# Four more chunks whose activations are turned by DMA: attention with pooled keys, then a mixture of adapters, on one core

## The chip, the cores and the metric

The kernel runs on 1 core of one Trainium2 chip. The metric is device microseconds (us) of that core, from one launch. The kernel before took 378.78 us, the median of 3 runs (378.42 to 379.87 us).

## The reference

Two stages follow each other. `q` has the shape (4, 12288, 128), `kv` (4, 384, 32, 128); the output has 49152 rows of 128.

```python
kv_pool = kv.reshape(B, H//4, 4, W//4, 4, C).mean(axis=(2, 4))   # 768 pooled rows per batch
k = v = kv_pool.reshape(B, -1, C) @ w_sr
a = softmax((q @ k.T) / sqrt(C))
x = (a @ v).reshape(B * S, D)                                    # stage 1
logits = x @ w_gate                                              # 8 experts, the top 2 of them
w = softmax over the two chosen logits
out = x + sum over the two chosen e of  w_e * (x @ A[e]) @ B[e]  # A: 128 x 16, B: 16 x 128
```

## The kernel before, in words

**Chunks and slots.** The 49152 queries are cut into 96 chunks of 512 (24 per batch). The main loop (lines 588 to 699) makes one pass per chunk; such a pass is called a slot here, and slot k is the pass with that value of `k`. The program keeps the order in which the code issues instructions on each engine, so the order in the code is the order in every queue. Several chunks are under way in a slot:

- three calls of `unit()`, the scores of chunk k (line 288): two matmuls of 512 columns each into PSUM, then one exponential on ScalarE (ACT);
- `attend` for chunk k-1 (line 306): 24 matmuls of 136 columns;
- `normalize` for chunk k-2 (line 323): a reciprocal and one multiplication on VectorE (DVE) give the rows `xn`; `top` and `route` start the choice of experts on DVE and GpSimd (POOL), and `gates` (line 373) ends it with a tanh on ACT and two products on POOL, `gw`;
- for an earlier chunk, found in `enter[k]`: `down` (line 427, four matmuls of 128 columns, `h_ps`, whose weights are the turned x), then `gate` (line 432, DVE, the gated activations `hg`);
- for the chunks in `ku`: `up` (line 441, four matmuls, `d_ps`, whose weights are the turned gated activations) and `finish` (line 450, an addition on DVE and the store to HBM, issued by SyncE, SP).

**Three ways to turn x and the gated activations.** Both products need their chunk with features on the partitions.

1. On TensorE (PE): `transposes` (line 381) uses four matmuls for x and four for the activations into one PSUM tile `tt_ps`, and DVE copies it to SBUF (`tts`, line 399).
2. `turn_h_dma` (line 422): the activations alone, by a DMA from `hs` to `ht`. The chunks in `by_queue` (line 542) take this way: the odd ones from 9 to 61. Their `up` comes six slots after their `gate` (line 677).
3. `turn_dma` (line 415), for the chunks in `by_dma` (line 338), 68 to 89: POOL narrows x to bf16 (`narrow`, line 412) in the slot in which the chunk is normalized, SP issues a DMA that turns it, and `down` uses it at the start of the slot two later. From the second chunk on the same DMA also turns the activations of another chunk. Slots in which the entering chunk is of this kind run through lines 604 to 636, which have no x transposes.

`by_dma` starts at `TURN` (line 336). Chunks before `TURN` are routed in pairs, those from `TURN` on one by one (`sizes`, line 337).

**The SP queue** issues, in the order of the code: the loads of `kv` (`load_kv`, line 97), the turning loads of the queries (`load_qT`, line 86: a DMA that turns 2048 rows of bf16 from HBM into SBUF, named `qT` or, for the last four groups, `qTs`), the stores of the output, and the DMAs of ways 2 and 3. SP handles them one after another. The queries in bf16 come from `cast_q` (line 79), a DMA from HBM to HBM that POOL issues. The slots of casts and query loads are written out by hand: `casts` (line 480, the groups 4 to 23 in order) and `loads` (line 481, slot to group; a group is 4 chunks, so group 17 holds the chunks 68 to 71). An odd slot with a `by_queue` chunk issues its load after that chunk's DMA (line 678), another slot just after its first `unit()` (line 601).

**PSUM.** `tt_ps`, `h_ps`, `d_ps` and the keys' tiles share two banks (`ps_m`, line 65).

**Other work in these slots.** The keys and values of the next batch are pooled by POOL (`add_patches`, line 495, at the end of the slots in `adds_at`) and made by the steps in `rest`, one per slot in which line 683 says so; for the last batch the last three are in the slots 69, 70 and 71. The kvr buffers of the pool `kvpool` also hold the last query groups and the strips of way 3 (`strip`, line 405).

Of the kernel before, what the change touches and what calls it, by code (L numbers as in the profile page):

```python
# [20 lines left out]
def kernel(  # L21
# [25 lines left out]
    NCHUNK = B * NB  # L47
# [21 lines left out]
    def mm(*a, **k):  # L69
        return keep(nc.tensor.matmul(*a, **k))  # L70
# [235 lines left out]
    def attend(k, s):  # L306
        b = k // NB
        if s == 0:
            acc[k] = ps_a.tile([P, S, 256], FP32, tag="acc", name="acc")
        o = acc[k][:, s, 0:VE]  # L310
        for j in range(J):
            mm(o, em[k][:, s, j], vx[b][:, j, 0:VE], start=(j == 0),
               stop=(j == J - 1))
# [19 lines left out]

    SOLO, TURN = NCHUNK - 6, NCHUNK - 28
    sizes = [1, 1] + [2] * (TURN // 2 - 1) + [1] * (NCHUNK - TURN)
    by_dma = range(TURN, SOLO)
    first, size = {}, {}
# [5 lines left out]
    def top(k):  # L345
        k0, m = first[k], k - first[k]
        if m == 0:
            srt[k0] = rpool.tile([P, GC, S, 8], FP32, tag="srt", name="srt")
        for s in range(S):
            keep(nc.vector.max(srt[k0][:, m, s], xn[k][:, s, C:C + E]))  # L350
# [3 lines left out]
    def route(k0):  # L354
        n = size[k0] * S
        eng = nc.gpsimd if k0 > 1 else nc.vector
        lg = xg[k0].rearrange("p m s c -> p (m s) c")[:, 0:n, C:C + E]
        so = srt[k0].rearrange("p m s e -> p (m s) e")[:, 0:n]

        def over(i):  # L360
            d = rpool.tile([P, GC * S, 8], FP32, tag=f"over{i}", name=f"over{i}")[:, 0:n]
            keep(eng.tensor_tensor(  # L362
                d, lg, so[:, :, i].unsqueeze(2).broadcast_to([P, n, 8]), op=ALU.subtract))
            return d

        arg, mask = over(0), over(1)
        keep(eng.tensor_tensor(arg, arg, mask, op=ALU.add))
        keep(eng.tensor_scalar(mask, mask, 0.0, None, op0=ALU.is_ge))  # L368


        later.append(lambda: gates(k0, n, eng, arg, mask))
# [55 lines left out]
    def down(k):  # L427
        hp[k] = mtile([P, S, P], name="h_ps")
        for s in range(S):
            mm(hp[k][:, s], xT[k][:, s], a_bf, start=(s == 0), stop=(s == S - 1))  # L430
# [44 lines left out]
    def unit(k=None, r=None):  # L475
        k, r = units.pop(0 if k is None else units.index((k, r)))
        scores(k, r)

    sums, rest = [], []
    casts = [8, 12, 15, 18, 20, 23, 26, 28, 31, 33, 36, 39, 41, 44, 46, 49, 51, 54, 57, 60]  # L480
    loads = {4 * g - 6: g for g in range(4, 18)}
    loads.update({57: 20, 59: 21, 61: 22, 64: 18, 65: 23, 66: 19})
    assert len(casts) == B * NG - 4

    rows_at, adds_at = {}, {}
    for b in range(2, B):
        for n in range(12):
            h, r, t = n // 4, n % 4, b * NB - 33 + 2 * n
# [6 lines left out]
    def add_patches(b, h, step, x):  # L495
        t = kvr[b, h]
        if step < 3:
            u, v = t[:, 0, x], t[:, step + 1, x]
        else:
            w = 2 * C if step == 3 else C  # L500
            u, v = t[:, 0, :, 0:w], t[:, 0, :, w:2 * w]
        keep(nc.gpsimd.tensor_tensor(u, u, v, op=ALU.add))  # L502

    def begin(k, queries=True):
        nonlocal sums, rest
        b, i = divmod(k, NB)
        g = k // GC
        if k in loads and queries:
            load_qT(loads[k])
        if k in casts:  # L510
            cast_q(4 + casts.index(k))
        if k in rows_at:
            load_kv(*rows_at[k], None)
        if i == 0 and 0 < b < B - 1:
            rest = prepare(b + 1, nc.gpsimd)[1]
        if k == 3:
            sums, rest = prepare(1, nc.gpsimd)
            sums = sum(sums, [])
        if 3 <= k < 15:
            load_kv(1, (k - 3) // 4, (k - 3) % 4, None)  # L520
        if k == 7:
            for _ in range(2):
                sums.pop(0)()

    def tanhs():
        while later:
            later.pop(0)()
# [7 lines left out]
    enter, t, left = {}, 1, list(range(NCHUNK - 3))  # L535
# [3 lines left out]
        left = [k for k in left if k not in enter[t]]  # L539
        t += 1  # L540

    by_queue = [k for t in range(13, TURN - 2) for k in enter[t] if k % 2]
    late_up = {}

    kh, ku, kd, kdone = [], [], [], []
# [42 lines left out]
    for k in range(k1, NCHUNK):  # L588
        b, i = divmod(k, NB)
        ka = att.get(k, [])  # L590
        kx = enter.get(k, [])
        begin(k, False)

        def after_norm(kn):
            top(kn)
            if kn == first[kn] + size[kn] - 1:
                route(first[kn])

        kn = [n for n in att.get(k - 1, []) if normed[n] == k]
        unit()  # L600
        if k in loads and not any(x_ in by_queue for x_ in kx):
            load_qT(loads[k])
        ku = ku + late_up.pop(k, [])
        if kx and not kd and all(x_ in by_dma for x_ in kx):
            down(kx[0])
            todo = []
            for n in kn:
                normalize(n)
                if n in by_dma:
                    narrow(n, k)  # L610
                    todo = [(xT, n)]
            tanhs()
            for h_ in kh:
                if h_ not in by_dma:
                    transposes(None, h_, nc.vector)
            unit()
            gate(kx[0], strip(k, 0)[:, 1])
            todo.append((hgT, kx[0]))
            if len(kx) == 1:
                turn_dma(k, *todo)  # L620
            for u_ in ku:
                up(u_)
                finish(u_)
            attend(ka[0], 0)
            attend(ka[0], 1)
            unit()
            for n in kn:
                after_norm(n)
            attend(ka[0], 2)
            for x_ in kx[1:]:  # L630
                down(x_)
                gate(x_, strip(k, 0)[:, 0])
                turn_dma(k, (hgT, x_), *todo)
            attend(ka[0], 3)
            kh, ku = kx, [c for c in kh if c not in by_queue]
            continue
        tanhs()
        for x_ in kd:
            down(x_)
        for n in kn:  # L640
            normalize(n)
            if n in by_dma:
                narrow(n, k)
                turn_dma(k, (xT, n))
        px = [c for c in kx if c not in by_dma]
        ph = [c for c in kh if c not in by_dma and c not in by_queue]
        pairs = [(px[j] if j < len(px) else None, ph[j] if j < len(ph) else None)
                 for j in range(max(len(px), len(ph)))]
        for x_, h_ in pairs[:1]:
            transposes(x_, h_, nc.vector)  # L650
        for x_ in kd:
            gate(x_)
        unit()
        for u_ in ku:
            up(u_)
            finish(u_)
        for a_ in ka[:-1]:
            for s in range(S):
                attend(a_, s)
            normalize(a_)  # L660
            after_norm(a_)
        if ka and len(ka) == 1:
            attend(ka[0], 0)
        for n in kn:
            after_norm(n)
        if k >= 13:
            unit()
            n0 = 1
        else:
            attend(ka[0], 1)  # L670
            n0 = 2
        for x_ in kx[:1]:
            down(x_)
            if x_ in by_queue:
                gate(x_, hpool.tile([P, S, P], BF16, tag="hs", name="hs"))
                turn_h_dma(x_)
                late_up[k + 6] = [x_]
                if k in loads:
                    load_qT(loads[k])
            else:  # L680
                gate(x_)
        kd = []
        if rest and i in ((14, 15, 16, 18, 19, 20, 21, 22, 23) if b == 0 else (5, 6, 7, 13, 14, 15, 21, 22, 23)):
            rest.pop(0)()
        for a_ in ka[-1:]:
            for s in range(n0 if len(ka) == 1 else 0, S):
                if s == S - 1:
                    for x_, h_ in pairs[1:]:
                        transposes(x_, h_, nc.scalar)
                        kd = [x_] if x_ is not None else []  # L690
                attend(a_, s)
        ku = [c for c in kh if c not in by_queue]
        kh = kx[:1] + kdone
        kdone = kd
        if k % 2 == 0 and 8 <= k <= 20:
            for _ in range(4 if k == 18 else 3):
                sums.pop(0)()
        for w in adds_at.get(k, []):
            add_patches(*w)
# [181 lines left out]
```

## Time and profile before

| what | before |
|---|---|
| median of 3 runs | 378.78 us |
| the profiled execution: its own time | 378.59 us |
| its span, first to last instruction | 376.8 us |
| busy share of TensorE, VectorE, ScalarE, GpSimd | 97%, 80%, 78%, 58% |
| mean granted TensorE clock | 0.993 |
| DMA moved | 85.75 MB, mean 228 GB/s |

The profile comes from one execution. Its span leaves out 1.8 us of the execution's own time, which lie before the first and after the last instruction. A page gives the busy time of each engine, the chain of work that ended last, and groups of instructions by line. The timeline lists single instructions of an engine with their start and duration in us; the windows view gives one row for a stretch. "SPq" rows are DMA issues by SyncE: the duration is that of the issue, not of the transfer. "PE" rows that overlap are pipelined, so the distance between two starts tells what a group costs.

### The profile page before, as it was taken

The page shows a single profiled execution, that of the slowest core. Times are in us where ns is not written, and L with a number is a line of the kernel's source. Part 1 is how long each engine was busy: PE and PEld are TensorE (multiplying, and loading weights), DVE is VectorE, ACT ScalarE, POOL GpSimd, SP SyncE. Part 2 cuts the span into 40 slices and gives each one's busy share as a digit, 9 for nine tenths or more (in the row PEclk, how much of TensorE's full clock was granted, in tenths as well). Part 3 has the DMA queues.
Part 4 walks back from the last instruction along what each step waited for, and adds up shares of the span by engine and source line. Part 5 has one row for each costly group of instructions (what it writes and reads, how often), then busy time and mean ns, then how long its engine had stood idle before and what let it go on. Part 6 is the DMA issues. An engine that isn't in the chain of part 4 may idle for free.

```text
span 376.8 us, 11335 instructions
## 1 busy us (share of the span) xinstructions
PE 365.9 (97%) x4340; PEld 287.5 (76%) x4340; DVE 300.5 (80%) x925; ACT 293.6 (78%) x368; POOL 218.2 (58%) x493
## 2 busy tenths in 40 slices
PE   8899999999999999999999999999999999999993
PEld 5667788877788787877877787787877777777782
DVE  1446799888888888888888888898898777777785
ACT  1548986787878788788878868877878999999873
POOL 0120368888766566557557566755645666666452
PEclk9999999999999999999999999999999999999997
DMA  8979669999999999999999999999875686777523
GB/s 255 397 261 218 231 176 271 298 268 255 240 288 265 185 288 312 182 241 294 240 259 249 287 275 203 204 257 243 211 211 156 169 170 170 169 151 186 143 88 139
DMA packets 66311, 85.75 MB, mean 228 GB/s; under 512 B 42736, under 2 KB 43504, under 8 KB 65904
## 3 DMA queue, kind: packets, MB, share of 16 engines
q1 hardware_dynamic: 62656, 73.29, 70.0%
q0 software_dynamic: 3168, 11.54, 18.2%
q8 instruction: 34, 0.56, 0.6%
q10 hardware_dynamic: 432, 0.20, 0.2%
q14 instruction: 21, 0.17, 0.2%
HBM read 50.53 MB, written 36.70 MB: 232 GB/s over the span
## 4 chain that ended last, share of the span: by engine, by line
PE 88%; DMA 6%; DVE 3%; ACT 1%; issue 1%; POOL 0%; SPq 0%; ACTq 0%; POOLq 0%
PE acc L70 35%; PE sg L70 32%; PE tt_ps L70 6%; PE d_ps L70 5%; PE h_ps L70 5%; DMA kvr<-in_kv_dram 4%; DMA qf<-in_q_dram 2%; PE v_ps L70 1%; PE kpT_ps L70 1%; DVE xn L330 1%; DVE tts L399 1%; DMA out_dram<-osb 1%; ACT em L304 1%; PE kfT_ps L70 0%; PE tail_ps L70 0%
## 5 line engine op out<-in xcount | busy, mean ns | idle before, releaser
L304 ACT ACTIVATE em<-sg 128x1024 f16<-128x1024 f32 x288 | 282.7, 1022 | 64.7 <-PE sg L70 62.0
L70 PE MATMUL acc<-vx,em 128*128 128x136 f16 x2280 | 166.5, 223 | 0.0
L70 PEld LDWEIGHTS <-em 128*128 128x128 f16 x2304 | 145.3, 98 | 8.2 <-DVE xn L330 0.6
L70 PE MATMUL sg<-qT,kfT 128*128 128x512 bf16 x480 | 142.0, 379 | 0.8 <-ACT em L304 0.7
L330 DVE TENSOR_TENSOR xn<-acc,rinv 128x540 f32<-128x540 f32 x95 | 68.4, 720 | 3.3
L452 DVE TENSOR_TENSOR osb<-d_ps,xn 128x512 f32<-128x512 f32 x91 | 62.4, 688 | 1.1
L362 POOL TENSOR_TENSOR over<-xn,srt 128x64 f32<-128x64 f32 (+1 forms) x120 | 30.9, 278 | 50.5 <-DVE srt L350 50.4
L502 POOL TENSOR_TENSOR kvr<-kvr 128x512 f32<-128x512 f32 (+1 forms) x48 | 56.9, 1201 | 0.5
L70 PEld LDWEIGHTS <-tts 128*128 128x128 bf16 x456 | 34.6, 97 | 25.4 <-issue 0.4
L70 PEld LDWEIGHTS <-kfT 128*128 128x128 bf16 x576 | 46.3, 98 | 4.5 <-issue 1.0
L377 POOL TENSOR_TENSOR gw<-th,over 128x64 f32<-128x64 f32 (+1 forms) x60 | 17.3, 289 | 51.7 <-ACT th L375 49.6
L325 DVE RECIPROCAL rinv<-acc 128x4 f32<-128x4 f32 x95 | 17.3, 182 | 36.1 <-PE acc L70 35.2
L399 DVE COPY tts<-tt_ps 128x1024 bf16<-128x1024 bf16 (+1 forms) x73 | 41.6, 569 | 0.0
L435 DVE TENSOR_TENSOR hg<-h_ps,gw 128x512 bf16<-128x512 f32 x44 | 30.4, 691 | 9.1 <-POOL gw L378 8.4
L70 PEld LDWEIGHTS <-xn 128*128 128x128 bf16 x296 | 22.6, 98 | 16.7 <-DVE xn L330 0.4
L350 DVE MAX8 srt<-xn 128x8 f32<-128x8 f32 x380 | 34.5, 153 | 0.1
L70 PE MATMUL sg<-qTs,kfT 128*128 128x512 bf16 x96 | 28.6, 379 | 0.0
L70 PE MATMUL tt_ps<-id_bf,xn 128*128 128x128 bf16 x284 | 27.4, 219 | 0.0
L70 PE MATMUL h_ps<-a_bf,tts 128*128 128x128 bf16 x284 | 27.4, 219 | 0.0
L368 POOL TENSOR_SCALAR over<-over 128x64 f32<-128x64 f32 (+1 forms) x60 | 19.8, 331 | 5.3
L225 POOL TENSOR_TENSOR kvr<-kvr 128x512 f32<-128x512 f32 x18 | 22.5, 1271 | 0.1
L70 PEld LDWEIGHTS <-turn 128*128 128x128 bf16 x176 | 13.4, 98 | 10.2 <-issue 0.2
(97 smaller groups left out, 318.4 us busy)
## 6 DMA issues: line engine op xcount, KB each, us to landing
out_dram<-osb SPq DMA_DIRECT2D x94, 256.0 KB, 4.0
kvr<-in_kv_dram SPq DMA_DIRECT2D x45, 512.0 KB, 6.5
qbf<-in_q_dram POOLq DMA_DIRECT2D x22, 512.0 KB, 8.1
qf<-in_q_dram SPq DMA_DIRECT2D x8, 256.0 KB, 7.6
kvr<-in_kv_dram SPq DMA_DIRECT2D x6, 256.0 KB, 7.6
ht<-hs SPq DMA_TRANSPOSE x27, 6.6
out_dram<-osb SPq DMA_DIRECT2D x3, 128.0 KB, 2.4
turn<-turn SPq DMA_TRANSPOSE x23, 3.1
```

Source lines behind the costliest of these rows:

```text
L70: return keep(nc.tensor.matmul(*a, **k))
L225: keep(adder.tensor_tensor(u[:, lo:hi], u[:, lo:hi], v[:, lo:hi], op=ALU.add))
L304: keep(nc.scalar.activation(o, i_, AF.Exp, bias=0.0, scale=scale))
L325: keep(nc.vector.reciprocal(ri, acc[k][:, :, VC]))
L330: keep(nc.vector.tensor_tensor(x[:, :, 0:VC], acc[k][:, :, 0:VC], ri.unsqueeze(2).broadcast_to([P, S, VC]), op=ALU.mult))
L350: keep(nc.vector.max(srt[k0][:, m, s], xn[k][:, s, C:C + E]))
L362: keep(eng.tensor_tensor(d, lg, so[:, :, i].unsqueeze(2).broadcast_to([P, n, 8]), op=ALU.subtract))
L368: keep(eng.tensor_scalar(mask, mask, 0.0, None, op0=ALU.is_ge))
L399: keep(nc.vector.tensor_copy(sb[:, lo:hi], ps[:, lo:hi]))
L435: keep(nc.vector.tensor_tensor(hg[k].rearrange("p s (e r) -> p (s e) r", e=E), hp[k].rearrange("p s (e r) -> p (s e) r", e=E), gw[k0][:, m ...
L452: keep(nc.vector.tensor_tensor(osb, dp[k], xn[k][:, :, 0:C], op=ALU.add))
L502: keep(nc.gpsimd.tensor_tensor(u, u, v, op=ALU.add))
```

## The change

`TURN` goes from 68 to 64, so the chunks 64 to 67 also take way 3, and `by_queue` is now the odd chunks from 9 to 63 (63 is new in it). The last query casts and query loads move to earlier slots. Two steps that the slots of lines 604 to 636 did not have, the key steps (`prepare_next`) and `add_patches`, are now called there too.

```diff
-    SOLO, TURN = NCHUNK - 6, NCHUNK - 28
+    SOLO, TURN = NCHUNK - 6, NCHUNK - 32
...
-    casts = [8, 12, 15, 18, 20, 23, 26, 28, 31, 33, 36, 39, 41, 44, 46, 49, 51, 54, 57, 60]
+    casts = [8, 12, 15, 18, 20, 22, 25, 27, 30, 32, 35, 37, 39, 42, 44, 47, 49, 52, 55, 57]
     loads = {4 * g - 6: g for g in range(4, 18)}
-    loads.update({57: 20, 59: 21, 61: 22, 64: 18, 65: 23, 66: 19})
+    loads.update({55: 20, 57: 21, 59: 22, 61: 18, 63: 23, 64: 19})
...
+    def prepare_next(b, i):
+        if rest and i in ((14, 15, 16, 18, 19, 20, 21, 22, 23) if b == 0 else (5, 6, 7, 13, 14, 15, 21, 22, 23)):
+            rest.pop(0)()
...
-    by_queue = [k for t in range(13, TURN - 2) for k in enter[t] if k % 2]
+    by_queue = range(9, TURN, 2)
...
             for h_ in kh:
-                if h_ not in by_dma:
+                if h_ not in by_dma and h_ not in by_queue:
                     transposes(None, h_, nc.vector)
...
             for n in kn:
                 after_norm(n)
+            prepare_next(b, i)
             attend(ka[0], 2)
...
             kh, ku = kx, [c for c in kh if c not in by_queue]
+            for w in adds_at.get(k, []):
+                add_patches(*w)
             continue
...
-        if rest and i in ((14, 15, 16, 18, 19, 20, 21, 22, 23) if b == 0 else (5, 6, 7, 13, 14, 15, 21, 22, 23)):
-            rest.pop(0)()
+        prepare_next(b, i)
```

By engine, the instructions of the built program change so: TensorE loses 36 transposes of 128x128 (16 of x, 20 of gated activations) and their weight loads; VectorE loses the five copies of `tt_ps`; GpSimd gains four narrowing copies and, since four chunks are routed one by one instead of in two pairs, twelve small routing instructions, ScalarE two tanhs; SyncE gains four `turn` transposes and one `ht` transpose.

## Prediction

> **What bounds the kernel now.** I read the page first, for the busy shares and the chain of work that ended last.
>
> ```profile
> span 376.8 us, 11335 instructions
> ...
> PE 365.9 (97%) x4340; PEld 287.5 (76%) x4340; DVE 300.5 (80%) x925; ACT 293.6 (78%) x368; POOL 218.2 (58%) x493
> ...
> PE 88%; DMA 6%; DVE 3%; ACT 1%; issue 1%; POOL 0%; SPq 0%; ACTq 0%; POOLq 0%
> ```
>
> TensorE holds 88% of the chain, so a matmul taken away shortens the run; and since it works in order, a wait that is put in front of it lengthens it. The change acts around the slots 66 to 73, so next I read TensorE's timeline there. A slot begins with the first `sg` of its three units. Slot 68 begins at 268.91 (the first slot that changes its path), slot 74 at 292.32, slot 75 at 295.48.
>
> ```profile
> 268.91 0.59 PE L70 MATMUL sg<-qT,kfT 128*128 128x512 bf16 x2
> ...
> 275.69 0.41 PE L70 MATMUL kpT_ps<-id_f,kvr 128*128 128x128 f32 x2
> ...
> 279.69 0.68 PE L70 MATMUL v_ps<-wext,kpT 128*128 128x135 f32 x4
> ...
> 281.70 0.39 PE L70 MATMUL tt_ps<-id_bf,xn 128*128 128x128 bf16 x4
> 281.93 0.39 PE L70 MATMUL tt_ps<-id_bf,hg 128*128 128x128 bf16 x4
> 282.15 0.59 PE L70 MATMUL sg<-qT,kfT 128*128 128x512 bf16 x2
> 282.58 0.39 PE L70 MATMUL d_ps<-b_bf,tts 128*128 128x128 bf16 x4
> 283.10 0.38 PE L70 MATMUL d_ps<-b_bf,ht 128*128 128x128 bf16 x4
> 283.32 0.52 PE L70 MATMUL acc<-vx,em 128*128 128x136 f16 x6
> ...
> 284.35 0.27 PE L70 MATMUL kfT_ps<-id_bf,vb 128*128 128x128 bf16 x2
> ...
> 292.32 0.59 PE L70 MATMUL sg<-qT,kfT 128*128 128x512 bf16 x2
> ...
> 295.48 0.59 PE L70 MATMUL sg<-qT,kfT 128*128 128x512 bf16 x2
> ```
>
> The reader is to see two things. A slot in which everything is turned by DMA costs 295.48 - 292.32 = 3.16 us, and the six slots 68 to 73 cost 292.32 - 268.91 = 23.41 us, which is 4.45 us more than six such slots (18.96). And TensorE has small gaps here: the first `d_ps` group stands 0.52 us ahead of the second, while a group of four costs 283.32 - 283.10 = 0.22; the missing 0.30 is a wait for one of the two shared PSUM banks.
>
> **Part 1: the transposes leave TensorE.** Eight cost 282.15 - 281.70 = 0.45 us, 0.056 each. 36 go: 36 x 0.056 = 2.0 us, all on the path. Of the 4.45 us, 2.0 are these, 0.44 are two extra `up` groups (the late odd chunks 59 and 61), at most 0.41 + 0.68 + 0.27 = 1.36 are the key steps, so at least 0.65 are waits. The key steps stay in the slots 69 to 71. The number of `up` groups in the six slots stays eight: that of 63 moves from slot 69 to slot 73. What can change is the waits. VectorE loses five copies of `tt_ps`, and the bank that they held; against it, `h_ps` and two `d_ps` groups follow each other closely in the slots 71 and 73, with two banks, so the 0.30 wait is met there too. At best all 0.65 go, at worst they double. I take 0.1 us saved: **part 1 gives -2.1 us**, between -1.4 and -2.7.
>
> **Part 2: GpSimd.** Four narrowing copies, twelve small routing instructions and `add_patches` in slot 68 instead of the same place in the old path; GpSimd is 58% busy. Its results are used a slot or more later. I take 0; if that cover went, the price would be the delay of a narrowing copy, which is a part of the next term.
>
> **Part 3: the SP queue, and the new wait.** The first turn of x, for chunk 64, stands in slot 66 and must have landed when `down` of chunk 64 begins, just after the first unit of slot 68: 268.91 + (282.58 - 282.15) = 269.34. TensorE works in order, so everything stands behind these four matmuls. So the question is when SP gets to it.
>
> ```profile
> 226.67 1.23 SPq L424 DMA_TRANSPOSE ht<-hs  x1
> 227.99 0.75 SPq L448 DMA_DIRECT2D out_dram<-osb  x1
> 228.79 0.56 SPq L104 DMA_DIRECT2D kvr<-in_kv_dram  x1
> 231.39 0.35 SPq L448 DMA_DIRECT2D out_dram<-osb  x1
> 232.40 1.77 SPq L424 DMA_TRANSPOSE ht<-hs  x1
> 234.34 5.69 SPq L93 DMA_TRANSPOSE qTs<-qbf  x1
> 240.13 3.40 SPq L93 DMA_TRANSPOSE qT<-qbf  x1
> ...
> 272.73 2.70 SPq L93 DMA_TRANSPOSE qT<-qbf  x1
> 275.52 2.82 SPq L448 DMA_DIRECT2D out_dram<-osb  x5
> 280.59 1.22 SPq L417 DMA_TRANSPOSE turn<-turn  x1
> ```
>
> ```profile
> L93 SPq DMA_TRANSPOSE qTs<-qbf x4: 2525/3449/5693, 234.3 to 270.1; - x4
> L93 SPq DMA_TRANSPOSE qT<-qbf x4: 2262/2726/3398, 240.1 to 272.7; - x4
> ```
>
> From 234.34 on SP issues without a pause to 278.34. The last query load (group 19) has its place in slot 66, which begins two slots before 268.91, so at 262.6 at the latest (two of 3.16), but is issued at 272.73: SP runs 10 us or more behind the code. It has just caught up when the first `turn` is due at 280.59. Nothing in that stretch was urgent. After the change the first `turn` is four slots earlier, the last six loads only two or so.
>
> In the new SP order, between the `ht` at 226.67 and the first `turn` stand exactly the instructions that stand between 227.99 and the end of the load at 272.73 now: eight query loads, five `ht`, three kv loads, ten stores. What is gained is SP's idle time, since the load of group 20 comes up right after that `ht`: 231.39 - 229.35 = 2.04 and 232.40 - 231.74 = 0.66, together 2.7 us. So the first `turn` is issued at about 275.52 - 2.7 = 272.8, where the loads take what they take now, 26.2 us for the eight (from the two rows of loads: least, greatest and twice the median of each four).
>
> Ends for that: all eight at the shortest, 2.26, is 18.1 us, and the issue comes at 264.7; two more of them at 5.69 instead of 3.40, as next to a cast, gives 277.4. The casts of the slots 57 and 60 become those of 55 and 57, so casts press on this stretch sooner, not more, and the mix of loads, kv, stores and `ht` is like now; I stay at 272.8. From issue to landing:
>
> ```profile
> DMA to landing us min/median/max: 2.4/3.1/4.5
> ```
>
> ```profile
> DMA to landing us min/median/max: 3.6/4.4/5.8
> ```
>
> The first row is that of all `turn`, in the quiet stretch after 280; the second that of the `ht` in the window 255 to 275, behind query loads. I take 3.7, between their medians: 276.5. **The wait is 276.5 - 269.3 = +7.2 us**; its ends are 0 (264.7 + 3.1 is before 269.3) and 277.4 + 4.4 - 269.3 = 12.5.
>
> What is late next: the `turn` of chunk 65 follows one store and its own 1.2 us of issue later, lands at some 279, and is needed one slot after the resumed one, at 279.7; that of the chunks 66 and 64 is bound by the gate after the wait and needed two slots on. Both fit, narrowly. I add nothing. The query load of group 17, which chunk 68 needs, now has group 18's in front of it. Between it and the first `turn` SP issues two loads, two `ht` and four stores: 2 x 2.7 + 2 x 1.8 + 4 x 0.56 = 11 us by these rows. So its issue ends by 262, 7 us before slot 68, and I cost it at nothing.
>
> The Trainium skill, page "DMA: Bandwidth & Descriptors", section "Issuing engines are not separate DMA queues", says that the sequencer's time to start a DMA is usually small beside the DMA itself. That speaks for no wait at all, my first rival below. The rows above disagree for these loads: their issue takes 2.3 to 5.7 us, and they sit in one queue.
>
> **Part 4: the clock after the wait.** TensorE runs at full clock in these slots, and at half when work gets thin:
>
> ```profile
> 1.21 3.59 PE L70 MATMUL spin_ps<-zero 128*128 128x512 bf16 x8 [1.21 <-DVE zero L179]
> ```
>
> ```profile
> 371.90:376.80 4.90, 0.37 (x2) 0.21 (x2) 1.00 (x3) 0.12 (x1) 0.00 (x0) 0.50 0.59 211
> ```
>
> The first row is eight matmuls of the size of an `sg` at the start: 3.59 / 8 = 0.45 us each, where a pair in slot 71 takes 0.43, so 0.22 each. The second row is the sparse tail, with 0.50 in the column of the granted clock. A wait of 7 us may bring the half clock back for a while. The cost is half the time spent in it: 0 if the clock stays, and 1.8 if the slow start comes back in full (3.59 / 2). The wait is long beside those, so I take a value nearer to the upper end, **+1.3 us**. By the Trainium skill, "TensorE: Matmul & The Clock Gate", Part 1, an idle window of about 3.4 us halves the clock and about 3.4 us of busy time restores it; an estimate from that page would be 1.7 us.
>
> **The sum**, against the profiled execution's own time of 378.59 us (span 376.8, and 1.8 outside of it; the median of the runs, 378.78, is 0.2 higher): 378.6 - 2.1 + 7.2 + 1.3 = **385.0 us**.
>
> **Rivals.**
>
> - *SP is in time.* If the loads' issue times shrink because they meet fewer casts, the first `turn` lands before 269.3 and only part 1 is left: 378.6 - 2.1 = 376.5 us. This is the case on the other side. It decides at an issue before 269.3 - 3.1 = 266.2, 6.6 us sooner than my walk. For it: a load can be issued in 2.26, and the casts end three slots earlier. Against it: the loads that met no cast still took 2.3 to 3.4, and SP's whole idle time is 2.7. Chance 0.14.
> - *A short wait.* Half of that is gained: issue at 269.5, landing at 272.6, wait 3.3, and no loss of clock worth counting: 379.8 us. Chance 0.15.
> - *Waits in a row.* The `turn` of 65, and that of 66 with 64, also come late by 2 us each, since SP has stores in front of them and DMA is still behind: 385.0 + 4 = 389 us. For it: the margins above are 1 us or less. Against it: after 275 the loads are over, and landings fall to 2.4 to 3.1. Chance 0.13.
> - That the transposes don't leave TensorE is excluded: the built program's order shows 36 fewer.
>
> **How the numbers follow.** My forecast, one long wait, has 0.58. Its own range, by an issue at 270.5 to 275 and the clock's ends, is 381.4 (wait 4.9, no loss of clock) to 387.7 (wait 9.4, loss 1.8). To hold 8 in 10 I reach over the short wait (379.8) below and to the waits in a row above: 379 to 389. What a measurement of this kernel can tell from no change is about 0.5%, 1.9 us. Faster by more than that (under 376.9) is most of the first rival: 0.11. Within it: the rest of that and about two thirds of the short wait: 0.12. Slower: 0.77.
>
> **What would show it.** In the changed profile: the six slots have no `tt_ps`, and slots of about 3.2 to 3.7 us (part 1); TensorE's timeline has one gap ahead of the first `h_ps` that reads `turn`, ended by a DMA (part 3), with SP's timeline showing that `turn` issued at 270 to 275, close behind the loads; the windows view has a granted clock under 1 just after it (part 4). Wrong it would be if SP pauses before that `turn`: then the loads got shorter. If the gap is there but stands at an `sg`, a query load was late instead.

## The result, and the profile after

The changed kernel took 399.76 us, the median of 6 runs (395.38 to 411.13); the kernel before, on the same chip, 378.97 us (378.42 to 379.87, 6 runs). The ratio is 1.0493, with a 95% interval of 1.043 to 1.0557: slower, by more than the 385.0 us forecast and outside the range. Here and below medians are over all runs, while ratios leave out runs over 1.5% above the fastest of their kernel, so a ratio can be smaller than that of the medians, and is missing where too few runs are left.

The profiled execution took 395.38 us. From its page: the span, the busy times, the granted clock in 40 slices, and the chain of work that ended last.

```profile
span 392.8 us, 11289 instructions
...
PE 367.0 (93%) x4298; PEld 286.6 (73%) x4304; DVE 297.9 (76%) x920; ACT 294.7 (75%) x370; POOL 223.1 (57%) x509
...
PEclk9999999999999999999999999999579999999997
...
PE 75%; DMA 16%; DVE 3%; SPq 2%; ACT 1%; issue 1%; POOL 0%; ACTq 0%; DVEq 0%; POOLq 0%
```

The page counts 4298 matmuls of TensorE instead of 4340 (36 of the 42 are the transposes; six `sg` are missing from the trace, 474 of 480), but its busy time did not fall (367.0 us against 365.9); its share of the chain went from 88% to 75%, and DMA's from 6% to 16%. There is a dip in the clock at three quarters of the span. TensorE's timeline there (start, duration, instructions, and in brackets the idle time before and what ended it):

```profile
273.37 0.61 PE L70 MATMUL sg<-qT,kfT 128*128 128x512 bf16 x2 [0.66 <-DMA qT<-qbf]
284.86 0.61 PE L70 MATMUL h_ps<-a_bf,turn 128*128 128x128 bf16 x4 [10.88 <-DMA turn<-turn]
285.26 1.06 PE L70 MATMUL sg<-qT,kfT 128*128 128x512 bf16 x2
...
289.95 0.59 PE L70 MATMUL sg<-qT,kfT 128*128 128x512 bf16 x2
...
293.33 0.59 PE L70 MATMUL sg<-qT,kfT 128*128 128x512 bf16 x2
...
307.94 0.59 PE L70 MATMUL sg<-qT,kfT 128*128 128x512 bf16 x2
```

Slot 68 begins at 273.37, slot 69 at 289.95, slot 74 at 307.94. One wait stands ahead of the first `h_ps` that reads `turn`, ended by its DMA, and the `sg` pair after it takes 1.06 us instead of 0.59. The spans differ by 392.8 - 376.8 = 16.0 us, and the starts give it in five terms:

| term | worked out | us |
|---|---|---|
| late at the start of slot 68 | 273.37 - 268.91 | +4.46 |
| the wait for the first `turn` | 284.86 - 273.37 - 0.43 (an `sg` pair) | +11.06 |
| rest of slot 68 at half clock | 289.95 - 284.86 = 5.09, against 2.73 at full clock (shown below) | +2.36 |
| slots 68 to 73 without these | 307.94 - 273.37 - 11.06 - 2.36 = 21.15, against 23.41 | -2.26 |
| from slot 74 to the end | 392.8 - 307.94 = 84.86, against 376.8 - 292.32 = 84.48 | +0.38 |

The first term was not forecast. The waits view of the changed kernel (us in total, times, longest) says what it is:

```profile
PEld L70 <- DMA turn<-turn: 12.1, 2, 11.4
PE h_ps L70 <- DMA turn<-turn: 11.4, 2, 10.9
...
PEld L70 <- DMA ht<-hs: 4.3, 4, 1.5
...
PE d_ps L70 <- DMA ht<-hs: 2.4, 4, 1.0
...
PEld L70 <- DMA qT<-qbf: 1.3, 2, 0.8
```

TensorE waits four times for an `ht`, between 150.8 and 233.9 us, long before slot 68, and twice for a query load: at 153.6 for that of group 9 and at the start of slot 68 for that of group 17. The kernel before has none of these. The six idle gaps add up to 3.3 us; at the same six places ScalarE's exponentials, which follow the `sg`, fall behind those of the kernel before by 4.25 us, so these waits make up nearly all of the +4.46. Both transfers come through SP, whose timeline in the changed kernel reads (start and duration of each issue):

```profile
139.24 11.04 SPq L93 DMA_TRANSPOSE qT<-qbf  x1
...
214.52 9.26 SPq L93 DMA_TRANSPOSE qT<-qbf  x1
...
239.27 1.29 SPq L424 DMA_TRANSPOSE ht<-hs  x1
240.72 3.90 SPq L93 DMA_TRANSPOSE qTs<-qbf  x1
...
277.21 2.59 SPq L93 DMA_TRANSPOSE qT<-qbf  x1
...
282.35 1.21 SPq L417 DMA_TRANSPOSE turn<-turn  x1
```

The `ht` of slot 55, here just ahead of the load of group 20, is issued at 239.27; in the kernel before the same `ht` was at 226.67. From there to the first `turn` it is 43.1 us, where the prediction had 272.8 - 226.67 = 46.1. So SP was not slow in the stretch that the prediction walked through: it came to that stretch 12.6 us late. All query loads of a kernel in one row each (duration of the issue in ns: least, median, greatest), first the kernel before, then the changed one:

```profile
L93 SPq DMA_TRANSPOSE qT<-qbf x18: 2262/4520/7503, 32.4 to 272.7; - x18
```

```profile
L93 SPq DMA_TRANSPOSE qT<-qbf x18: 2417/5180/11045, 32.4 to 277.2; - x18
```

The issues of all 22 loads (with the four `qTs`) add up to 95.0 us before and 116.0 us after. They are the same loads of the same size. The windows view of the stretch in which the first long ones stand, the kernel before and then the changed one (the last two columns are the busy share of the DMA engines, which can pass 1 since a packet counts where it starts, and GB/s):

```profile
100.00:150.00 50.00, 50.00 (x620) 39.82 (x618) 43.44 (x131) 39.53 (x49) 32.16 (x60) 1.00 1.09 269
```

```profile
100.00:150.00 50.00, 49.78 (x612) 39.34 (x609) 43.43 (x130) 39.56 (x49) 32.31 (x61) 1.00 1.09 202
```

The DMA engines are busy throughout in both, but move less in the changed kernel, not more.

### The profile page after: what moved, and what is told of

It is laid out like the page before. It is cut to its first block, busy times and chain, and to the rows that moved or that the text cites. A ratio compares the mean times of both kernels' runs of the same rounds, so it can differ in the third digit from the quotient of the medians.

```text
span 392.8 us, 11289 instructions
## 1 busy us (share of the span) xinstructions
PE 367.0 (93%) x4298; PEld 286.6 (73%) x4304; DVE 297.9 (76%) x920; ACT 294.7 (75%) x370; POOL 223.1 (57%) x509
## 4 chain that ended last, share of the span: by engine, by line
PE 75%; DMA 16%; DVE 3%; SPq 2%; ACT 1%; issue 1%; POOL 0%; ACTq 0%; DVEq 0%; POOLq 0%
PE acc L70 31%; PE sg L70 27%; DMA ht<-hs 9%; DMA kvr<-in_kv_dram 6%; PE tt_ps L70 5%; PE d_ps L70 5%; PE h_ps L70 5%; DMA turn<-turn 2%; SPq L93 1%; PE v_ps L70 1%; DVE xn L330 1%; PE kpT_ps L70 1%; ACT em L304 0%; SPq L424 0%; PE tail_ps L70 0%
## 5 line engine op out<-in xcount | busy, mean ns | idle before, releaser
L70 PEld LDWEIGHTS <-tts 128*128 128x128 bf16 x420 | 32.1, 98 | 23.3 <-issue 0.6
L399 DVE COPY tts<-tt_ps 128x1024 bf16<-128x1024 bf16 (+1 forms) x68 | 38.4, 565 | 0.2 <-PE tt_ps L70 0.2
L435 DVE TENSOR_TENSOR hg<-h_ps,gw 128x512 bf16<-128x512 f32 x39 | 27.0, 691 | 8.7 <-POOL gw L378 8.2
L70 PEld LDWEIGHTS <-turn 128*128 128x128 bf16 x208 | 15.9, 98 | 23.9 <-DMA turn<-turn 12.1
L70 PEld LDWEIGHTS <-xn 128*128 128x128 bf16 x280 | 21.3, 98 | 15.7 <-DVE xn L330 0.4
L435 DVE TENSOR_TENSOR turn<-h_ps,gw 128x512 bf16<-128x512 f32 x26 | 17.7, 682 | 13.4 <-PE h_ps L70 13.2
L70 PE MATMUL tt_ps<-id_bf,xn 128*128 128x128 bf16 x268 | 25.9, 219 | 0.0
L70 PE MATMUL h_ps<-a_bf,tts 128*128 128x128 bf16 x268 | 25.8, 219 | 0.0
```

The source lines that it names most:

```text
L399: keep(nc.vector.tensor_copy(sb[:, lo:hi], ps[:, lo:hi]))
L435: keep(nc.vector.tensor_tensor(hg[k].rearrange("p s (e r) -> p (s e) r", e=E), hp[k].rearrange("p s (e r) -> p (s e) r", e=E), gw[k0][:, m ...
```

## The experiments

**Two theories.** *A:* the moved casts cost: they lengthen the issues of the loads on SP, and so the first `turn`, and some `ht`, come late. *B:* it is the place of the first `turn` behind SP's queue alone, and the wait of 10 us and more is what `TURN` = 64 costs. In each experiment the kernel before ran beside it, at medians of 378.5 to 378.8 us.

### The change taken apart

`casts_only` is the kernel before with the new casts:

```diff
-    casts = [8, 12, 15, 18, 20, 23, 26, 28, 31, 33, 36, 39, 41, 44, 46, 49, 51, 54, 57, 60]
+    casts = [8, 12, 15, 18, 20, 22, 25, 27, 30, 32, 35, 37, 39, 42, 44, 47, 49, 52, 55, 57]
```

> The kernel before with the new list of casts alone; query loads and TURN stay. Theory A (the denser casts lengthen the issues of the query loads on SP, and the ht transposes behind them come late): the waits of TensorE for ht in the slots 36 to 58 are there, 3.6 us in the changed kernel, and the eight-odd loads between 95 and 230 us take about 20 us more of issue; 382 to 388 us. Rival B (the lag of SP comes from the earlier query loads and the turns, the casts cost nothing, as the prediction had it): no ht waits, 378 to 380 us.

Measured: 378.79 us (377.88 to 394.81, 10 runs), ratio 0.9988 (0.9959 to 1.0018). In the median the casts cost nothing, as B expected; but four of the ten runs took 383.8 to 394.8, while none of the 13 of the kernel before beside them took over 382.50. The trace, of a run of 378.11, has loads of 101.2 us in sum and no wait for `ht`; none of the four long runs was traced, so what lengthened them is open.

`after_old_casts` is the changed kernel with the old casts, the edit above the other way round:

```diff
-    casts = [8, 12, 15, 18, 20, 22, 25, 27, 30, 32, 35, 37, 39, 42, 44, 47, 49, 52, 55, 57]
+    casts = [8, 12, 15, 18, 20, 23, 26, 28, 31, 33, 36, 39, 41, 44, 46, 49, 51, 54, 57, 60]
```

> The changed kernel with the old list of casts; the loads stay moved and TURN stays 64. Theory A: no ht waits before slot 58, the first turn issued at about 273 us as the prediction's walk had it, a wait for it of 5 to 8 us, 383 to 388 us. Rival B: the lag is as in the changed kernel, the wait 11 us, 391 us or more.

Measured: 392.85 us (385.56 to 395.79, 4 runs; no ratio). The trace, of the longest run, has the wait at `turn` (11.10 us), two waits for query loads (0.62 and 1.80), one for an `ht` (0.35), and loads of 112.7 us in sum. This is what B expected; but one of the four runs took 385.56, and the same kernel, run again below, gave the answer of A.

`turn_alone` puts the old loads back as well, so that only `TURN` and the steps of the other path are changed:

```diff
-    loads.update({55: 20, 57: 21, 59: 22, 61: 18, 63: 23, 64: 19})
+    loads.update({57: 20, 59: 21, 61: 22, 64: 18, 65: 23, 66: 19})
```

> TURN = 64 and the steps in the other path alone; casts and query loads as before. If the place of the first turn behind the loads on SP is what costs: the same loads stand in front of it, three of them two slots later in the code but on a queue that lags anyway, so the wait is 6 to 9 us and the time 384 to 389 us. If the earlier loads had been of use, clearly more than the changed kernel with old casts; if they were of none, the same within 1 us.

Measured: 387.47 us (386.31 to 389.76, 4 runs), ratio 1.0231 (1.0196 to 1.0267). `TURN` alone brings some 9 us, most of it the wait at the first `turn`: 10.70 us in the run of 389.76, where 6 to 9 were expected.

`after_old_loads` is the changed kernel with that edit alone, new casts and old loads:

```diff
-    loads.update({55: 20, 57: 21, 59: 22, 61: 18, 63: 23, 64: 19})
+    loads.update({57: 20, 59: 21, 61: 22, 64: 18, 65: 23, 66: 19})
```

> The changed kernel with the old query loads: TURN = 64 and the new casts. If the casts alone cost at the first turn what separates the changed kernel from the one with its casts undone, about 395; if the earlier loads are what pushes the needed ones back (16 behind 21, 17 behind 18), the time is that of TURN = 64 alone, 386 to 389 us, and TensorE has no wait for a query load.

Measured: 394.51 us (385.04 to 405.1, 4 runs; no ratio). Loads 122.1 us in sum, two waits for `ht` of 0.54 and 1.38 us, 11.98 us at `turn`: near the 395 that were expected if the casts alone cost, though one of the four runs took 385.04.

These first results are wide apart and not all of one chip, so all four were run again together on one chip. `changed_again` is the changed kernel, and the other three are `turn_alone`, `after_old_casts` and `after_old_loads` under new labels, without a further edit.

> The changed kernel again, beside the three that undo a part of it, on one chip. If denser casts and earlier loads add up on the SP queue: the slowest of the four, 394 to 402 us, with TensorE waits for ht before slot 58 and 11 us or more for the first turn. If the gap to the others was chance of one day or chip: within 3 us of them.

> TURN = 64 alone, again, on the same chip as the three others: the fastest of the four, 385 to 389 us, in both views.

> The changed kernel with the old casts, again: if the earlier loads alone cost, by the needed loads 16 and 17 standing behind 21 and 18, 3 us or more over TURN = 64 alone, with a TensorE wait for a query load; if not, within 1.5 us of it.

> The changed kernel with the old loads, again: if the denser casts alone cost once the first turn is early, 4 us or more over TURN = 64 alone, with loads of 8 us and more from 95 to 230 us; if their cost is chance, within 1.5 us of it.

| kernel (all with `TURN` = 64) | first time, us | second time, one chip, us | ratio, second time | loads' issues in sum, the two traces |
|---|---|---|---|---|
| old casts, old loads | 387.47 | 388.7 (386.81 to 390.54) | 1.025 (1.0207 to 1.0294) | 104.5, 99.1 |
| old casts, new loads | 392.85 | 386.48 (385.42 to 387.81) | 1.0196 (1.0158 to 1.0234) | 112.7, 98.5 |
| new casts, old loads | 394.51 | 392.98 (384.29 to 401.38) | 1.0175 (1.011 to 1.0239) | 122.1, 120.4 |
| new casts, new loads | 399.76 | 400.8 (394.54 to 405.08) | 1.0503 (1.0433 to 1.0574) | 116.0, 127.7 |

The second time, with the old casts the earlier loads cost nothing (386.48 us against 388.7, though `turn_alone_2` was expected to be the fastest of the four); the first time they had seemed to cost 5.4 us. With the new loads the new casts bring 14.3 us by the medians, and the ratios agree: 1.0503 against 1.0196, with intervals that lie apart. With the old loads it is open: the medians are 4.3 us apart, but the ratios are 1.0175 with the new casts and 1.025 without, since two of the six runs with them took 384.29 and 387.25. (By the medians of the first time the casts bring 7.0 us with the old loads and 6.9 with the new ones.) The sum of the loads' issues goes with the time of the traced runs: 98 to 105 us in the three under 390 us, 113 to 128 in the five over it. Theory B falls as the whole story: `TURN` gives half of the loss. Theory A holds with `TURN` = 64 and the new loads; without `TURN` = 64 the median does not move.

The kernel with the new loads and the old casts (`old_casts_2`) is the one whose start of the stretch is like that of the kernel before. Its SP and TensorE timelines:

```profile
228.95 1.25 SPq L424 DMA_TRANSPOSE ht<-hs  x1
230.37 3.72 SPq L93 DMA_TRANSPOSE qTs<-qbf  x1
...
274.10 1.21 SPq L417 DMA_TRANSPOSE turn<-turn  x1
```

```profile
268.79 0.59 PE L70 MATMUL sg<-qT,kfT 128*128 128x512 bf16 x2
276.66 0.61 PE L70 MATMUL h_ps<-a_bf,turn 128*128 128x128 bf16 x4 [7.28 <-DMA turn<-turn]
...
281.47 0.59 PE L70 MATMUL sg<-qT,kfT 128*128 128x512 bf16 x2
```

There the first `turn` is issued at 274.10 and the wait is 7.28 us. The run took 385.42 us. But the casts don't settle the start alone. The same `ht` in `after_old_casts`, also with the old casts, and in `changed_again`, the changed kernel again:

```profile
235.27 1.27 SPq L424 DMA_TRANSPOSE ht<-hs  x1
```

```profile
245.20 1.74 SPq L424 DMA_TRANSPOSE ht<-hs  x1
```

So it was issued at 228.95 and 235.27 with the old casts, at 239.27 and 245.20 with the new ones. And the worst, `changed_again` (a run of 402.59), in its waits:

```profile
PEld L70 <- DMA ht<-hs: 8.9, 6, 2.5
...
PEld L70 <- DMA qT<-qbf: 5.5, 4, 2.0
```

### The queue ahead of the first turn

The first four of these start from `turn_alone`. If the queue on SP is what delays the first `turn`, work taken out of it must bring that forward; if the DMA engines are simply full, whatever SP's order, the wait stays near 10 us. `loads_spread` moves six loads behind the first turns:

```diff
-    loads.update({57: 20, 59: 21, 61: 22, 64: 18, 65: 23, 66: 19})
+    loads.update({68: 18, 72: 19, 76: 20, 80: 21, 84: 22, 88: 23})
...
-        if k in loads and not any(x_ in by_queue for x_ in kx):
+        if k in loads and not any(x_ in by_queue or x_ in by_dma for x_ in kx):
...
             if len(kx) == 1:
                 turn_dma(k, *todo)
+            if k in loads:
+                load_qT(loads[k])
```

> TURN = 64, old casts; the query loads of the groups 18 to 23 go to the slots 68, 72, 76, 80, 84 and 88, each just behind that slot's turn on SP, so that no more than the loads of 16 and 17 are near the first turn. SP-queue theory: no wait for the first turn, TensorE keeps its clock, and part 1 of the prediction is left, 376 to 378 us, up to 381 if each later load pushes a turn late by 0.5 us. Rival (DMA itself is full at that time, whatever SP's order): a wait of 4 us or more for the first turn stays, 382 us or more.

Measured: 383.51 us (382.39 to 386.13, 4 runs), ratio 1.0147 (1.0101 to 1.0192). The first `turn` is issued at 265.52 and there is no wait for it; the time is still over the 381 that were expected at most, since the loads now stand ahead of later turns. Waits view, and the two longest of these waits in TensorE's timeline:

```profile
PE h_ps L70 <- DMA turn<-turn: 4.3, 5, 1.7
```

```profile
274.71 0.40 PE L70 MATMUL h_ps<-a_bf,turn 128*128 128x128 bf16 x4 [1.66 <-DMA turn<-turn]
...
283.71 0.40 PE L70 MATMUL h_ps<-a_bf,turn 128*128 128x128 bf16 x4 [1.35 <-DMA turn<-turn]
```

`two_loads_behind` moves only the groups 19 and 23, by the same code:

```diff
-    loads.update({57: 20, 59: 21, 61: 22, 64: 18, 65: 23, 66: 19})
+    loads.update({57: 20, 59: 21, 61: 22, 64: 18, 68: 19, 70: 23})
```

> TURN = 64 alone, with the loads of the groups 19 and 23 moved to the slots 68 and 70, just behind these slots' turns on SP. SP-queue theory: two issues of 2.4 and 2.9 us leave the queue before the first turn, the wait falls by about 5 to 5 to 6 us, 382 to 384 us. Rival (DMA engines full): the wait stays, 386 to 388 us.

Measured: 382.09 us (381.06 to 387.36, 10 runs), ratio 1.0088 (1.0059 to 1.0117). The first `turn` is issued at 270.62, the wait is 3.87.

`stores_on_act` takes 18 stores out of SP's queue:

```diff
-        store(nc.sync, k, osb)
+        store(nc.scalar if 46 <= k <= 63 else nc.sync, k, osb)
```

> TURN = 64 alone, with the stores of the chunks 46 to 63 issued by ScalarE instead of SP. SP-queue theory: some 12 stores at 0.55 us leave the stretch before the first turn, and issues in front of it get room, so the wait shrinks from 10.7 to 3 to 5 us; 380 to 383 us. Rival (the 16 DMA engines are what is full, and SP's issue only shows it): the wait stays within 2 us of what it was, 386 to 388 us.

Measured: 383.65 us (383.44 to 388.68, 4 runs), ratio 1.0153 (1.0073 to 1.0232). Issue at 271.63, wait 4.55. With the whole queue the issue was at 277.25 (`turn_alone`), 276.18 (`turn_alone_2`) and 274.50 (`wait_with_spins`, below), so it came 2.9 us ahead of the earliest of these. The stores still run, issued from elsewhere, so at least these 2.9 us are SP's queue and not full DMA engines. `stores_and_loads` makes the last two edits together.

> TURN = 64 with old casts, with both reliefs of SP together: the stores of the chunks 46 to 63 issued by ScalarE, and the loads of groups 19 and 23 behind the turns of the slots 68 and 70. Each alone moved the first turn 5 to 7 us forward. SP-queue theory: together the first turn is issued before 267, TensorE does not wait, the clock stays, and part 1 (2.2 us) is left, less about 0.6 for the two loads among the turns: 376.5 to 378 us, just faster than before or the same. Rival (part of the wait is of the DMA engines and does not go): a wait of 2 us or more, 380 us or more.

Measured: 381.30 us (381.06 to 388.26, 6 runs), ratio 1.0072 (1.0056 to 1.0088). The first `turn` is issued at 266.78 and lands in time; what was hoped for beyond that did not come. TensorE's and GpSimd's timelines show the next link:

```profile
270.18 0.39 PE L70 MATMUL h_ps<-a_bf,turn 128*128 128x128 bf16 x4
274.91 0.40 PE L70 MATMUL h_ps<-a_bf,turn 128*128 128x128 bf16 x4 [1.41 <-DMA turn<-turn]
```

```profile
266.77 0.29 POOL L368 TENSOR_SCALAR over<-over 128x32 f32<-128x32 f32 x1
267.02 2.50 POOL L502 TENSOR_TENSOR kvr<-kvr 128x512 f32<-128x512 f32 x2
...
270.01 0.61 POOL L413 CAST turn<-xn 128x512 bf16<-128x512 f32 x1
```

The narrowing copy of chunk 65 stands behind two additions of `add_patches`, 2.50 us, and its `turn` comes late.

`four_reliefs` takes that copy and that of chunk 66 to VectorE, and puts the two loads further back:

```diff
-        keep(nc.gpsimd.tensor_copy(strip(t, 0)[:, 0], xn[k][:, :, 0:C]))
+        keep((nc.vector if TURN < k < TURN + 3 else nc.gpsimd).tensor_copy(strip(t, 0)[:, 0], xn[k][:, :, 0:C]))
...
-    loads.update({57: 20, 59: 21, 61: 22, 64: 18, 68: 19, 70: 23})
+    loads.update({57: 20, 59: 21, 61: 22, 64: 18, 71: 19, 80: 23})
```

> TURN = 64 with the casts of the kernel before, the stores of chunks 46 to 63 issued by ScalarE, the narrowing copies of chunks 65 and 66 on VectorE instead of GpSimd, and the query loads of the groups 19 and 23 in the slots 71 and 80, behind the early turns. If the first turn's place behind SP and then the narrowing copy on GpSimd are all that eats part 1, no wait over 0.5 us is left in the slots 68 to 73 and 377 to 378.5 us come out, up to 1.5 under the kernel before. If the next link is late in its turn (the gates of VectorE behind two more copies, or a load among the turns), 379 to 382 as with stores and loads moved alone.

Measured: 383.06 us (378.86 to 391.31, 12 runs), ratio 1.0049 (1.002 to 1.0079). The trace, of a run of 380.11, has no wait for a `turn` in the slots 68 to 73. Its waits view:

```profile
PEld L70 <- DMA turn<-turn: 1.9, 2, 1.1
...
PE sg L70 <- ACT em L304: 1.3, 3, 0.7
...
PEld L70 <- DVE tts L399: 1.1, 1, 1.1
```

What part 1 gains is given back in small pieces: ScalarE, which now issues stores, is late with an exponential (an `sg` pair waits 0.36 us for it, a store having been issued just ahead of it); VectorE, which now narrows, is late with a `tts` (a narrowing copy of 1.27 us stands ahead of it); a late `turn` waits behind a load. The runs fall into two groups, six from 378.86 to 381.91 and six from 384.22 to 391.31; only one of the first was traced, and what the others met is open. `reliefs_new_casts` is the same with the new casts.

> The same with the changed kernel's denser casts. If these cost by the longer issues of the query loads on SP, with the early turn behind them, then with SP relieved most of the cost is hidden again: within 2 us of the run with the old casts, with some waits for ht before slot 58 left. If denser casts cost by themselves, wherever the turns stand, 4 to 12 us more than with the old casts, as between TURN = 64 alone and the changed kernel.

Measured: 380.88 us (379.36 to 395.5, 7 runs), ratio 1.0035 (1.0021 to 1.0049); loads 99.2 us in sum, no wait for `ht`. So the new casts cost nothing by themselves here, by the ratios; two of the seven runs took 393.31 and 395.50. No version with `TURN` = 64 beat the kernel before.

### The clock after the wait

`wait_with_spins` is `turn_alone` with 44 idle matmuls ahead of the first `h_ps` that reads `turn`, which fill the wait; the output is unchanged.

```diff
+            if k == TURN + 4:
+                spin(44)
             down(kx[0])
```

> The kernel with TURN = 64 alone (old casts, old loads), with 44 idle matmuls of 512 columns, some 9.5 us, put before down of chunk 64 in slot 68, where TensorE waited 10.7 us. Clock theory (the wait halves the clock for 5 us and that costs 2.3): no stretch at half clock, the part of slot 68 behind the wait takes 2.7 us instead of 5.1, and the time falls by about 2.3 to 385 us. Rival (the slow slot comes from something else behind the wait): no change, 387.5 us.

Measured: 388.07 us (385.85 to 389.89, 4 runs), ratio 1.0235 (1.0168 to 1.0301): no shorter than `turn_alone`, so the expected fall to 385 did not come. In the trace the spins ended 1.5 us after the `turn` had landed, which gives back part of the gain, and the issue of the `turn` differs between runs. What the clock costs is read from the slot. First `turn_alone`, then `wait_with_spins`, from `h_ps` to the next slot:

```profile
280.08 0.61 PE L70 MATMUL h_ps<-a_bf,turn 128*128 128x128 bf16 x4 [10.70 <-DMA turn<-turn]
...
285.15 0.59 PE L70 MATMUL sg<-qT,kfT 128*128 128x512 bf16 x2
```

```profile
269.38 9.67 PE L70 MATMUL spin_ps<-zero 128*128 128x512 bf16 x44
278.89 0.38 PE L70 MATMUL h_ps<-a_bf,turn 128*128 128x128 bf16 x4
...
281.62 0.60 PE L70 MATMUL sg<-qT,kfT 128*128 128x512 bf16 x2
```

285.15 - 280.08 = 5.07 us at half clock, 281.62 - 278.89 = 2.73 where the clock stayed: 2.34 us.

### What lengthens the loads

`before_again` is the kernel before, unchanged, for a second trace.

> The kernel before, unchanged, for a second trace of it. In all traces with TURN = 64 so far some query loads between 185 and 235 us took 8 to 13 us of issue; in the first trace of before, and in the run with the new casts alone, none there took more than 6.3. If that is chance from run to run, such a load can turn up here too, without any wait of TensorE (the ht have six slots of room): 378 to 380 us either way. If it comes with TURN = 64, the loads here take 3.9 to 6.3 us again.

Measured: 378.04 us, one run. Loads 95.2 us in sum, as in the first trace (95.0).

`casts_denser` is the kernel before with casts in every second slot from 20 to 50:

```diff
-    casts = [8, 12, 15, 18, 20, 23, 26, 28, 31, 33, 36, 39, 41, 44, 46, 49, 51, 54, 57, 60]
+    casts = [8, 12, 15, 18] + list(range(20, 52, 2))
```

> The kernel before with casts every second slot from 20 to 50, denser than in the change (about every 2.5). Theory A (denser casts lengthen the query loads' issues and make ht late): loads of 8 us and more in the stretch of the casts, waits of TensorE for ht, 382 to 400 us. Rival (the moved casts do nothing): 378 to 380 us, loads of 4 to 7 us.

Measured: median 379.05 us of 10 runs from 378.51 (two at 387.45 and 387.70, and one stray of 967.55; the kernel before beside it had a stray of 761.89), ratio 1.0007 (0.9996 to 1.0018). Its loads:

```profile
L93 SPq DMA_TRANSPOSE qT<-qbf x18: 2422/6526/8729, 31.4 to 269.2; - x18
```

113.4 us in sum, a median of 6.5 us instead of 4.5, and no wait of TensorE for an `ht` or a load: with the first `turn` in its old place, four slots later, SP's lag is hidden. But none of these loads is longer than 8.7 us, and from 100 to 150 us DMA moved 279 GB/s here. So this run shows longer loads beside more casts, but not the loads of 10 us and more in a stretch of 202 GB/s.

The loads over all traces: with the old casts, 11 of 12 have 95 to 106 us in sum, one 112.7; with denser casts, five of seven have 113 to 128, two (`casts_only`, `reliefs_new_casts`) 99 to 101. So denser casts make long loads likely and not certain. **Open** is what decides it from run to run: up to the store of chunk 46 SP's order is the same in all these kernels. The two short ones with denser casts are both of one chip, so the chip may have a part in it; on the chip of the second time all four kernels ran, and there the sums were 99.1 and 98.5 us with the old casts, 120.4 and 127.7 with the new ones. Also untested is whether the casts' number in a stretch counts or their place beside the loads: the new list puts a cast into the slots 22, 30 and 42, in which a query load stands, the old one into 26, 46 and 54.

## Why the prediction was wrong in size and right in direction

- **Part 1, transposes (-2.1):** right, -2.26, where the half clock is taken out with the 2.73 us of `wait_with_spins`.
- **Part 2, GpSimd (0):** right in the changed kernel, where SP is later still. It named its price rightly: once SP is relieved, the delay of a narrowing copy is the next wait (1.41 us in `stores_and_loads`).
- **Part 3, the walk along SP:** the place and the cause are as told: one gap ahead of the first `h_ps` that reads `turn`, ended by that DMA, with the `turn` issued just behind the loads. The step that failed is its start: it began at the `ht` of 226.67, "casts press on this stretch sooner, not more", and so costed the moved casts, and any lag of SP at that `ht`, at nothing. It looked at the stretch behind that `ht`; the casts were also drawn together ahead of it (the last 16 span the slots 20 to 57 instead of 20 to 60), where the issues of loads grew to as much as 11.0 us, and SP came to the same `ht` at 239.27, 12.6 us late. That the moved casts are a cause is shown by the two kernels with the new loads on one chip (400.8 us against 386.48); how they lengthen the loads, and why not in every run, stays open, and with the old casts too the start was once 8.6 us late (235.27). Where it was only 2.3 us late, at 228.95, the rest of the walk came out: issue 274.10 (272.8 told), landing 276.62 (276.5), wait 7.28 (7.2), time 385.42 in the trace and 386.48 in the median (385.0). That the landing fits so closely is luck: the issue was 1.3 us later than told, and the landing took 2.5 us instead of 3.7.
- **The stretch itself:** 46.1 us told; 43.1 (`after`), 45.2 (`old_casts_2`, 274.10 - 228.95), 45.3 (`changed_again`) and 47.5 (`after_old_casts`) measured.
- **What is late next:** the `turn` of 65 fitted, as told. The load of group 17 did not: its issue was to end by 262, 7 us ahead of slot 68, but ended at 271.6, and chunk 68's `sg` waited 0.66.
- **Not in the sum:** the `ht`, which have six slots of room, and for which TensorE waited four times in the changed kernel. With the two query loads this is nearly all of the +4.46.
- **Part 4, the clock (+1.3, at most 1.8):** too small: 2.36, and 2.34 in the pair made for it. The upper end, half of the eight spins' 3.59 us at the start, was not a bound. The windows view of the changed kernel (the stretch, its length, the busy time and instructions of PE, PEld, DVE, ACT and POOL, then the granted clock, the DMA share and GB/s):

```profile
276.10:284.80 8.70, 0.00 (x0) 0.00 (x0) 0.00 (x0) 0.00 (x0) 0.00 (x0) 0.50 0.60 162
284.80:289.75 4.95, 4.89 (x33) 3.79 (x34) 1.66 (x6) 1.78 (x2) 1.75 (x5) 0.50 0.91 182
289.75:293.20 3.45, 3.45 (x44) 2.77 (x42) 2.76 (x9) 2.89 (x5) 2.80 (x8) 1.00 0.44 127
```

  The half clock goes on for 4.9 us after work has come back, so it costs half of that.
- **The rivals:** none came true. "SP is in time" needed an issue before 266.2; in `loads_spread`, issued at 265.52, the first wait is indeed gone. "Waits in a row" named another mechanism than that which brought the time over it. The range ended at 389 since no term let SP's lag at the start of the walk grow; the traces of before, with loads of up to 7.5 us, gave a row to do it with.

## What to carry to other kernels

A queue that handles its instructions one after another is to be walked from the last point at which it was surely idle, not from where the edit begins: whatever was moved ahead of that point shifts the whole walk. A lag that costs nothing today (SP was 10 us behind and its loads varied in length) is priced by the earliest consumer, and an edit that brings a consumer forward turns every variation of that lag into waits of the engine that bounds. Where one wait is taken away, look which engine feeds the next: here SP, then GpSimd, then ScalarE and VectorE gave back all of a gain of 2.3 us. And one trace per kernel is not enough where a queue's lag varies: the same kernel gave 392.85 us and 386.48 on two chips, with a wait of 11.10 us in one trace and 7.28 in the other.

## What the runs showed of the hardware that was not expected

- The issue of a turning load of 2048 rows from HBM held SP for 2.3 to 13.1 us within one run; that of a turn within SBUF took 1.2 us (the `turn` at 282.35 above). The row of `old_loads_2`:

```profile
L93 SPq DMA_TRANSPOSE qT<-qbf x18: 2263/5786/13112, 31.8 to 278.2; - x18
```

By the Trainium skill, "DMA: Bandwidth & Descriptors", section "Issuing engines are not separate DMA queues", only the sequencer's time is saved by issuing elsewhere, usually little. It was not little here: in `stores_on_act`, with 18 stores issued elsewhere, TensorE waited 4.55 us instead of 9.61 to 10.70 in the two traces of `turn_alone`'s kernel, and the median was 3.8 us lower than `turn_alone`'s, though the intervals of the two ratios overlap.
- The half clock lasts in whole steps: by the clock's records 3.41 us in `stores_on_act`, 6.83 in `old_casts_2`, 10.24 in `turn_alone`, 13.65 in the changed kernel. This agrees with the free-running window of 3413 ns that the Trainium skill, "TensorE: Matmul & The Clock Gate", Part 1, states. In all four the clock came back at the end of the first whole step that lay behind the return of the work (in the changed kernel work returned at 284.86, and the last step ran from 286.34 to 289.75), so with the clock already at half, a return costs half of 3.41 us and half of what is left of the step before. (In `old_loads_2`, with 10.24 us, the last step began 0.04 us before the return.)
